# One port for two engines: a list scheduler that charges VectorE and GpSimd operations to a common resource

## The chip, the cores and the metric

The program runs on 1 core of one Trainium2 chip. A core has five engines with a queue of its own each: TensorE (PE in the rows, its weight loads PEld), VectorE (DVE), ScalarE (ACT), GpSimd (POOL) and SyncE (SP), which here only issues DMAs. Each engine takes its instructions in the order in which they stand in its queue. The metric is the device time of one execution in microseconds (us), the median of three runs.

## The reference

The kernel computes three blocks one after the other, on 4 batches of 576 tokens (2304 tokens), in fp32:

```python
A = sm(q, k_lm); Bm = sm(q_lm, k_lm); C = sm(q_lm, k)     # landmark attention, 8 heads of 64, 32 landmarks
Z = Bm^T / (norm1(Bm) * norminf(Bm) + 1e-6)
for _ in range(6): Z = 2 * Z - Z @ Bm @ Z
x = (A @ Z @ C @ v)                                        # [2304, 512]
h = x @ w_in;  x = max(0.01 * h, h) @ w_out                # first block: 512 -> 2048 -> 512
xn = x / sqrt(mean(x * x) + 1e-6) * rms_g                  # second block: 512 -> 1536 -> 512
g = xn @ w_gate; out = (silu(g) * (xn @ w_val)) @ w_out2
```

The weights arrive as 64-bit floats and are turned into fp32 on the chip.

## The kernel before

TensorE multiplies in a reduced fp32 form, so every operand is split into a high part (a rounded copy) and a low part (operand minus high part), and every product is made of three: high x high, low x high, high x low. The low parts are subtractions of two operands in SBUF; they and other elementwise work can be done by VectorE or by GpSimd.

**First block.** 8 half batches of 288 tokens (j) times 16 blocks of 128 hidden columns (f) are 128 units. `ffn1_h` makes one unit's hidden block with 6 matmuls into `ph` (line 739; the attention's last product is folded into the weights by `form_m`, line 706), ScalarE writes its high part `g_hi` (L755) and an fp32 copy `hs` (L758), and the subtraction at L761 gives the low part `g_lo`. `ffn1_y` then adds the unit to the output with 12 matmuls into `py` (L797), which wait for `g_lo`. Finished half batches go to DRAM (`y_dram`).

**Between the blocks.** `norm` loads a half batch `y_in`, squares it, sums over the 512 values (L925, L927, then a matmul at L932), takes the reciprocal root (`rr`, L938 to L952, the power on GpSimd at L943), spreads it with a matmul (`dg`, L957, L962), scales (L968) and writes it back. `prep_x` loads it again and makes seven combinations of its quarters (`tx`, L1001 to L1017) with their high and low parts (L313 and L862). `prep_w` does the same for each block of the gate and value weights (`cg`, `tt`, L890 to L897). `convert` (L337 to L400) turns a 64-bit weight piece `raw` into fp32 in three steps, the last at L374 (`cg<-raw`, `ct<-raw`) on VectorE.

**Second block.** 12 blocks of 128 hidden columns times 4 batches are 48 units (`gv`), each of seven products of 6 matmuls (L1034), by Strassen's scheme in Winograd's form. The sums of the products are five VectorE additions with an operand in PSUM: `g_hi` (L1087), `g_lo` (L1090, L1093), `ys` (L1100, L1123). TensorE's sixth product of a unit waits for L1090, its seventh for L1093. ScalarE applies Silu, and two multiplications `us` (L1108) go to DRAM. At the end 18 output tiles of 36 matmuls each (L1189) are made from `us` and `w_out2`, whose converted form comes back from DRAM as `ct` (L1149).

**What sets the order.** Every piece of work is a Python generator that yields a list of options, (engine, ns), and the events and free buffers that it needs. `Order.run` (L109) is a list scheduler: it keeps for each engine the time at which it becomes free, takes the tasks that can begin within 100 ns of the earliest, and among these the one with the smallest sum of weighted begin and due time. Where a step has several options, it takes the engine with the smallest end plus `bias`. So the order of all five queues and the choice between VectorE and GpSimd come from the lengths in `pe`, `act`, `dve`, `pool` (L152 to L181), from `bias`, and from the due times made of `unit`, `unit2` and `prep` in `PAR` (L26). The chip runs the queues in that order; semaphores make each instruction wait for its operands.

Of the kernel before, what the change touches and what calls it, by code (L numbers as in the profile page):

```python
# [26 lines left out]
    "bias": {"dve": 300, "act": 0, "pool": -700},  # L27
# [3 lines left out]
    "unit": 1900,  # L31
# [13 lines left out]
    "unit2": 2500,  # L45
    "prep": 9000,
# [3 lines left out]
class Order:  # L50
# [7 lines left out]
    GAP = 110  # L58

# [6 lines left out]
    def add(self, due, length, gen):  # L66

        task = [due - length, 0, gen, None]
        task[3] = next(gen)
        self.tasks.append(task)  # L70

    def aside(self, gen):

        self.tasks.append([self.task[0], self.now, gen, next(gen)])
        self.branches.append(self.tasks[-1])
# [33 lines left out]
    def run(self):  # L109
        while self.tasks:  # L110
            able = []
            for task in self.tasks:
                options, needs = task[3]
                t = self.ready(needs)
                if t is not None:
                    t = max(t, task[1])
                    starts = [max(t, self.engines.get(e, 0)) for e, _ in options]
# [12 lines left out]
            try:  # L130
                task[3] = task[2].send(engine)
# [4 lines left out]
            if engine is not None:  # L136
                self.engines[engine] = t + ns
            t += ns + self.GAP
            task[0] += ns + self.GAP
# [12 lines left out]
def pe(n, count=1):  # L152
    return [("pe", int(count * (n / 2.4 + 3)))]
# [13 lines left out]

def dve2(n):
    return [("dve", int(n * 0.52) + 68)]
# [6 lines left out]
def pool_dve(n):  # L176
    return pool(n) + dve(n)
# [11 lines left out]
def landmark_attention_then_two_ffns(  # L189
# [134 lines left out]
    raws, gv_f32, p2 = {}, {}, {}  # L324

# [11 lines left out]
    def convert(k, key):  # L337
# [14 lines left out]
        e = yield [("pool", 590)] + act(490) + dve2(512), []  # L352
# [14 lines left out]
        yield dve(512), room  # L367
        if what == "in":
            t = w_in_sb[f // NP][:, f % NP, :]
        else:  # L370
            tag, home = ("cg", p2["a"]) if what in ("gate", "val") else ("ct", conv)
            ct = new(tag, home, [P, 512], U32)
            t = ct[:]
# [23 lines left out]
        e = yield pool(512) + dve(512), []  # L397
# [55 lines left out]
    def chain(b, g):  # L453
# [36 lines left out]
        yield dve(2), []  # L490
# [13 lines left out]
        yield dve(2), []  # L504
        nc.vector.tensor_scalar_add(sm, sm, EPS_SM)
        rs = att_tile([P, 2], "rs")
        yield dve(2), []
        nc.vector.reciprocal(rs, sm)
        bb = att_tile([P, 2, M], "bb")
        yield dve(M + 45), []  # L510
# [7 lines left out]
        yield dve(2 * M), []  # L518
# [9 lines left out]
        yield dve(60), []  # L528
# [3 lines left out]
        yield dve(1), []  # L532
        nc.vector.tensor_scalar_add(al[:, 2:3], al[:, 2:3], -EPS_Z)
        yield dve(1), []
# [3 lines left out]
        yield dve(M + 45), []  # L538
# [99 lines left out]
    def soft_a(b, g, h):  # L638
# [25 lines left out]
        e = yield pool(SB - 60) + dve(SB), []  # L664
# [5 lines left out]
        yield dve(nb), []  # L670
        nc.vector.tensor_scalar_add(st[:, 0, :], st[:, 0, :], EPS_SM)
        yield dve(nb + 30), []
        nc.vector.reciprocal(st[:, 1, :], st[:, 0, :])
        e = yield pool(SB - 60) + dve(SB), []
# [8 lines left out]
        e = yield pool(SB) + dve(SB), []  # L683
# [41 lines left out]
    def ffn1_h(u):  # L725
# [34 lines left out]
        e = yield pool(SB) + dve(SB), []  # L760
# [95 lines left out]
    def split_steps(parts):  # L856

        for hi, lo, src, n in parts:
            e = yield act(n) + dve2(n), []
            copy(e, hi, src)  # L860
            e = yield pool(n) + dve(n), []
# [45 lines left out]
    def norm(j):  # L907
# [7 lines left out]
        e = yield act(SB) + dve(SB), [("tt", 2)]  # L915
        ss = [new("tt", p2["a"], [P, 2, SB]) for _ in range(2)]
        for d in range(KD):
            if d:
                e = yield act(SB) + dve(SB), []
# [25 lines left out]
        yield dve(3), []  # L945
        nc.vector.tensor_mul(rr[:, 2, :], rr[:, 1, :], rr[:, 1, :])
        yield dve(3), []
# [3 lines left out]
        yield dve(3), []  # L951
# [3 lines left out]
        yield dve(SB), []  # L955
# [407 lines left out]
```

## Time and profile before

| | |
|---|---|
| median of 3 runs | 917.7 us (915.56 to 921.79) |
| the profiled execution itself | 918.04 us, of which the span of the trace is 916.3 us |
| busy | PE 845.9, DVE 484.4, ACT 319.2, POOL 477.3 us |
| instructions | 6416 matmuls, 932 on VectorE, 777 on ScalarE, 476 on GpSimd |
| first block's last matmul ends, by the trace | near 453 us |
| output tiles begin, by the trace | near 763 us |

A line of waits names the waiting engine and line, the one that released it, the total in us, the number of times and the longest. Busy time of VectorE and GpSimd includes what an instruction spends waiting for something inside the engine after it has begun.

### The profile page before, as it was taken

What the parts mean: (1) busy time and instruction counts of PE and PEld (TensorE: products, weight loads), DVE (VectorE), ACT (ScalarE), POOL (GpSimd) and SP (SyncE); (2) the same over time, 40 slices, a digit from 0 to 9 for tenths busy, and PEclk for the clock granted to TensorE, in tenths of its full rate; (3) what the DMA queues carried; (4) which work ended last, traced back from release to release, by engine and by line L of the source; (5) the groups of instructions that cost most, each with busy time, mean ns of one, the idle gap of its engine ahead of it and who ended that gap; (6) DMA issues with size and microseconds to landing.
All of it is one profiled execution on the core that took longest, in us unless ns stands there. A gap on an engine that the chain in (4) does not pass through costs nothing.

```text
span 916.3 us, 16631 instructions
## 1 busy us (share of the span) xinstructions
PE 845.9 (92%) x6416; PEld 747.5 (82%) x6416; DVE 484.4 (53%) x932; ACT 319.2 (35%) x777; POOL 477.3 (52%) x476
## 2 busy tenths in 40 slices
PE   3898999999999999898866999999999979999998
PEld 1577798988888778888866999999999978888886
DVE  6983751132316515687766866666667564242420
ACT  3674543342434435544332333333332341000000
POOL 2865752322425426767455766666665556364550
PEclk8899999999999999999988999999999999999999
DMA  9957741113103105655313344444342254534330
GB/s 321 331 190 217 218 153 52 53 53 95 37 1 105 53 1 181 207 187 185 127 67 117 92 162 132 133 133 133 132 133 87 76 190 140 172 104 152 113 104 34
DMA packets 63694, 118.51 MB, mean 129 GB/s; under 512 B 5504, under 2 KB 36224, under 8 KB 63616
## 3 DMA queue, kind: packets, MB, share of 16 engines
q1 hardware_dynamic: 63616, 117.46, 39.1%
q8 instruction: 50, 0.82, 0.4%
q14 instruction: 28, 0.23, 0.1%
HBM read 81.27 MB, written 36.18 MB: 128 GB/s over the span
## 4 chain that ended last, share of the span: by engine, by line
PE 66%; DVE 15%; DMA 9%; issue 3%; POOL 3%; ACT 3%; SPq 1%; DVEq 0%; ACTq 0%; POOLq 0%
PE py L797 16%; PE py L1189 15%; PE py L1034 11%; PE ph L739 8%; PE ph L1034 5%; PE pa L1034 3%; PE pa L706 3%; DMA ct<-wo_dram 2%; DVE tt L897 2%; DVE cg L374 1%; DMA y_dram<-ys 1%; DMA raw<-w_val 1%; DMA y_in<-y_dram 1%; DVE w L862 1%; DMA raw<-w_in 1%
## 5 line engine op out<-in xcount | busy, mean ns | idle before, releaser
L797 PE MATMUL py<-g_hi,w 128*128 128x288 f32 x1024 | 211.4, 299 | 0.1
L761 POOL TENSOR_TENSOR g_lo<-hs,g_hi 128x288 fp32r<-128x288 f32 x118 | 100.2, 851 | 155.4 <-ACT hs L758 134.3
L797 PEld LDWEIGHTS py<-g_hi,w 128*128 128x128 f32 x1024 | 164.7, 189 | 7.0 <-issue 3.5
L797 PE MATMUL py<-g_lo,w 128*128 128x288 f32 x512 | 151.7, 296 | 0.0
L739 PE MATMUL ph<-at,mm 128*128 128x288 f32 x768 | 128.6, 304 | 8.6 <-ACT hs L758 6.9
L739 PEld LDWEIGHTS ph<-at,mm 128*128 128x128 f32 x768 | 108.1, 189 | 30.0 <-ACT hs L758 12.7
L755 ACT ACTIVATE g_hi<-ph 128x288 fp32r<-128x288 f32 x128 | 52.4, 409 | 141.3 <-PE py L797 127.6
L797 PEld LDWEIGHTS py<-g_lo,w 128*128 128x128 f32 x512 | 97.2, 190 | 0.2 <-POOL g_lo L761 0.2
L1108 POOL TENSOR_TENSOR us<-hs,ys 128x288 f32<-128x288 f32 x47 | 46.3, 985 | 63.3 <-ACT hs L1097 26.0
L716 DVE TENSOR_TENSOR mm<-pa,mm 128x512 fp32r<-128x512 f32 x32 | 22.0, 688 | 70.7 <-ACT mm L311 70.5
L311 ACT COPY us<-py 128x512 f32<-128x512 f32 x18 | 10.6, 588 | 133.2 <-PE py L1189 133.2
L348 ACT ACTIVATE raw<-raw 128x512 f32<-128x512 f32 x52 | 35.5, 682 | 61.4 <-DMA raw<-w_out 20.6
L1189 PE MATMUL py<-q,w 128*128 128x512 f32 x240 | 56.1, 389 | 0.0
L1034 PE MATMUL py<-w,wt 128*128 128x288 f32 x288 | 44.5, 304 | 11.7 <-DVE g_lo L1090 10.9
L358 POOL TENSOR_SCALAR raw<-raw 128x512 uint32<-128x512 uint16 x45 | 31.6, 702 | 43.1 <-DMA raw<-w_out 13.0
L862 POOL TENSOR_TENSOR w<-w,w 128x768 fp32r<-128x768 f32 x18 | 36.4, 2049 | 31.7 <-DVE w L313 31.7
L1189 PEld LDWEIGHTS py<-q,w 128*128 128x128 f32 x240 | 45.0, 188 | 9.5
L758 ACT ACTIVATE hs<-ph 128x288 f32<-128x288 f32 x128 | 52.2, 408 | 0.0
L1034 PEld LDWEIGHTS py<-w,wt 128*128 128x128 f32 x288 | 40.8, 194 | 13.2 <-DVE g_lo L1090 12.1
L1108 POOL TENSOR_TENSOR us<-ys,g_lo 128x288 f32<-128x288 f32 x47 | 44.5, 947 | 8.8 <-ACT ys L1126 8.8
L862 POOL TENSOR_TENSOR at<-w,mm 128x768 fp32r<-128x768 f32 x16 | 32.0, 2030 | 29.7 <-DVE mm L313 29.7
L1034 PE MATMUL py<-w,mm 128*128 128x288 f32 x288 | 42.9, 297 | 3.3 <-DVE g_lo L1090 3.2
(263 smaller groups left out, 1746.9 us busy)
## 6 DMA issues: line engine op xcount, KB each, us to landing
u_dram<-us SPq DMA_DIRECT2D x48, 288.0 KB, 2.5
w<-u_dram SPq DMA_DIRECT2D x9, 1536.0 KB, 7.1
raw<-w_out SPq DMA_DIRECT2D x20, 512.0 KB, 4.1
y_dram<-ys SPq DMA_DIRECT2D x64, 144.0 KB, 1.9
y_in<-y_dram SPq DMA_DIRECT2D x16, 576.0 KB, 4.2
raw<-w_gate SPq DMA_DIRECT2D x12, 512.0 KB, 4.7
raw<-w_val SPq DMA_DIRECT2D x12, 512.0 KB, 4.0
kt<-kT SPq DMA_DIRECT2D x16, 288.0 KB, 4.5
```

The costliest lines, as they stand in the source:

```text
L348: nc.scalar.activation(high.bitcast(F32), high.bitcast(F32), AF.Prelu, scale=2.0 ** -112, alpha=2.0 ** 32)
L358: nc.gpsimd.tensor_scalar(low, upper, 2.0 ** -13, -0.5 + 2.0 ** -14, op0=ALU.mult, op1=ALU.add)
L706: nc.tensor.matmul(pm[lm, :], wt_in[b, g][rows, p], w_in_sb[c][rows, 2 * g + p, :].bitcast(F32), start=True, stop=True,)
L739: nc.tensor.matmul(ph[:, :SB], w[b, c][:, g, o:o + P], x[j][:, g, :], start=(n == 0), stop=(n == 3 * NG - 1),)
L755: nc.scalar.activation(g_hi[u], ph[:, :SB], AF.Prelu, alpha=0.01)
L758: nc.scalar.activation(hs, ph[:, :SB], AF.Prelu, alpha=0.01)
L761: engine[e].tensor_sub(g_lo[u], hs, g_hi[u].bitcast(F32))
L797: nc.tensor.matmul(yacc[i][d][:, :SB], w[f][:, d * P:(d + 1) * P], x[u], start=(f == f0 and n == 0), stop=(f == f1 - 1 and n == 2),)
L862: engine[e].tensor_sub(lo, src, hi.bitcast(F32))
L1034: nc.tensor.matmul(pp[:, :SB], w[f][:, i, c * P:(c + 1) * P], x[b][1][:, k, c, :], start=(first and n == 0), stop=(n == 5), skip_group_che ...
L1108: engine[e].tensor_mul(us[0][:, h, :], sg, t[name])
L1189: nc.tensor.matmul(po[:, :DM], x[n][1][:, f, m], w[f], start=(f == 0 and i == 0), stop=(f == NF2 - 1 and i == 2),)
```

## The change

1. The scheduler gets a resource `port`. `USES` says that a step on `"pool"` or on the new kind `"dvep"` holds its engine and the port; a plain `"dve"` step holds VectorE alone. `dvep` is VectorE work without a PSUM operand (and not a reduction or transpose); it is written in place of `dve` at some 30 steps.
2. `pe` counts 0.4375 ns a column and 6.5 ns a matmul, in place of 1/2.4 and 3. A PE step that follows a PE step of the same task needs no gap of 110 ns.
3. `bias` goes from +300 (VectorE), -700 (GpSimd) to 0 and -300; `unit` from 1900 to 2400, `unit2` from 2500 to 5600, `prep` from 9000 to 7000; `convert`'s second step counts 740 ns on GpSimd and 530 on ScalarE in place of 590 and 490.
4. Gate and value pieces must be converted in the order of `gv_keys`.

```diff
-    "bias": {"dve": 300, "act": 0, "pool": -700},
+    "bias": {"dve": 0, "act": 0, "pool": -300},
-    "unit": 1900,
+    "unit": 2400,
-    "unit2": 2500,
-    "prep": 9000,
+    "unit2": 5600,
+    "prep": 7000,
+    USES = {"dvep": ("dve", "port"), "pool": ("pool", "port")}
...
-                    t = max(t, task[1])
-                    starts = [max(t, self.engines.get(e, 0)) for e, _ in options]
+                    t = max(t, task[1] - (self.GAP if task[4] == "pe" == options[0][0] else 0))
+                    starts = [
+                        max(t, *(self.engines.get(r, 0) for r in self.USES.get(e, (e,))))
+                        for e, _ in options
+                    ]
...
             if engine is not None:
-                self.engines[engine] = t + ns
+                for r in self.USES.get(engine, (engine,)):
+                    self.engines[r] = t + ns
...
-    return [("pe", int(count * (n / 2.4 + 3)))]
+    return [("pe", int(count * (n * 0.4375 + 6.5)))]
...
+def dvep(n):
+    return [("dvep", int(n * 1.04) + 67)]
 def dve2(n):
-    return [("dve", int(n * 0.52) + 68)]
+    return [("dvep", int(n * 0.52) + 68)]
 def pool_dve(n):
-    return pool(n) + dve(n)
+    return pool(n) + dvep(n)
...
-        e = yield [("pool", 590)] + act(490) + dve2(512), []
+        e = yield [("pool", 740)] + act(530) + dve2(512), []
...
-        yield dve(512), room
+        if what in ("gate", "val"):
+            if key in gv_keys[1:]:
+                room.append("cg{},{}".format(*gv_keys[gv_keys.index(key) - 1]))
+        yield dvep(512), room
...
-        e = yield pool(SB) + dve(SB), []
+        e = yield pool(SB) + dvep(SB), []
         engine[e].tensor_sub(g_lo[u], hs, g_hi[u].bitcast(F32))
```

The mathematics, the tiles and the number of matmuls stay. In the built programs 307 instructions move from GpSimd (481 to 174) and 17 from ScalarE to VectorE (934 to 1258), counted over the whole order. Of the 128 subtractions at L761, VectorE gets 106 in place of 10; of the 96 `us` products at L1108, 95 in place of 2; of the 34 low parts of 768 columns on GpSimd at the end (L862), all 34. Lines of the changed kernel that stand behind line 360 carry a number 16 higher (L761 is L777, L1090 is L1106, L374 is L390, L1108 is L1124, L862 is L878); the copies at L313 are L324.

**Where it moves, first place: VectorE in the steady part of the second block.** One unit is the five additions from `g_hi` to the second `ys`; `cg<-raw` are the conversions of the next weights, `us` the products with Silu's result. Before:

```order
L1100 TENSOR_TENSOR ys<-g_hi,py 128x288
L1123 TENSOR_TENSOR ys<-g_hi,py 128x288
L374 SCALAR_TENSOR_TENSOR cg<-raw 128x512 x2
L1087 TENSOR_TENSOR g_hi<-hs,pa 128x288
L1090 TENSOR_TENSOR g_lo<-g_hi,py 128x288
L1093 TENSOR_TENSOR g_lo<-g_lo,py 128x288
```

Now:

```order
L1139 TENSOR_TENSOR ys<-g_hi,py 128x288
L878 TENSOR_TENSOR mm<-tt,mm 128x512
L1124 TENSOR_TENSOR us<-ys,g_lo 128x288
L1103 TENSOR_TENSOR g_hi<-hs,pa 128x288
L390 SCALAR_TENSOR_TENSOR cg<-raw 128x512
L1106 TENSOR_TENSOR g_lo<-g_hi,py 128x288
L390 SCALAR_TENSOR_TENSOR cg<-raw 128x512
L1109 TENSOR_TENSOR g_lo<-g_lo,py 128x288
```

The two conversions stood together ahead of a unit's first addition; now one stands behind the first and one behind the second, and the `us` products that GpSimd did are in VectorE's queue.

**Second place: the low parts `g_lo` of the first block while the second is being prepared.** Before, on GpSimd, near the preparation of the first batch (`tx`, `q`):

```order
L1001 TENSOR_TENSOR tx<-y_in 128x576
L862 TENSOR_TENSOR q_4551<-y_in,q_4550 128x576
L358 TENSOR_SCALAR raw<-raw 128x512
L761 TENSOR_TENSOR g_lo<-hs,g_hi 128x288
L862 TENSOR_TENSOR q_4551<-tx,q_4550 128x576
```

Now, on VectorE:

```order
L390 SCALAR_TENSOR_TENSOR cg<-raw 128x512 x2
L777 TENSOR_TENSOR g_lo<-hs,g_hi 128x288
L1017 TENSOR_TENSOR tx<-y_in 128x576
L324 CAST q_4567<-y_in 128x576 x2
L777 TENSOR_TENSOR g_lo<-hs,g_hi 128x288
L1033 TENSOR_TENSOR tx<-y_in 128x576
L878 TENSOR_TENSOR q_4568<-y_in,q_4567 128x576 x3
L777 TENSOR_TENSOR g_lo<-hs,g_hi 128x288
```

The low parts that TensorE waits for now stand in one queue with the combinations of `y_in`, which wait for DMAs.

**Third place: VectorE in the last units of the second block**, where `ct` comes from DRAM and `w` is a piece of `us` loaded back. Before:

```order
L1090 TENSOR_TENSOR g_lo<-g_hi,py 128x288
L313 CAST w_989<-w_121 128x768
L1108 TENSOR_TENSOR us<-ys,g_lo 128x288
L862 TENSOR_TENSOR w_989<-w_121,w_989 128x768
L1093 TENSOR_TENSOR g_lo<-g_lo,py 128x288
```

Now:

```order
L1103 TENSOR_TENSOR g_hi<-hs,pa 128x288
L324 CAST q_4567<-ct 128x512
L1106 TENSOR_TENSOR g_lo<-g_hi,py 128x288
L1109 TENSOR_TENSOR g_lo<-g_lo,py 128x288
L878 TENSOR_TENSOR q_4568<-ct,q_4567 128x512
```

The three instructions between the two additions `g_lo` are gone from there, and copies of `ct`, which wait for a DMA, stand ahead of one of them.

## Rows read from the trace of the kernel before

**Rows 1.** The page, busy us by engine (share of the span) and instructions.

```profile
PE 845.9 (92%) x6416; PEld 747.5 (82%) x6416; DVE 484.4 (53%) x932; ACT 319.2 (35%) x777; POOL 477.3 (52%) x476
```

**Rows 2.** Busy time by stretch: length, busy by engine, clock, DMA share, GB/s.

```profile
525.50:713.70 188.20, 180.80 (x1335) 177.30 (x1334) 128.29 (x226) 62.41 (x137) 118.44 (x126) 1.00 0.39 128
366.20:454.80 88.60, 77.55 (x556) 74.08 (x555) 64.83 (x113) 39.34 (x101) 59.18 (x53) 0.98 0.53 170
454.80:525.50 70.70, 53.55 (x360) 52.27 (x360) 49.88 (x75) 22.78 (x48) 40.73 (x35) 0.88 0.30 103
713.70:771.10 57.40, 52.61 (x356) 50.16 (x354) 30.52 (x56) 18.36 (x39) 30.95 (x29) 0.97 0.48 157
0.00:366.20 366.20, 339.85 (x3206) 278.50 (x3207) 170.93 (x438) 165.74 (x436) 165.44 (x204) 0.98 0.40 129
```

**Rows 3.** TensorE's waits from 525.5 to 713.7: total us, times, longest.

```profile
PE py L1034 <- DVE g_lo L1090: 7.4, 9, 1.1
```

**Rows 4.** TensorE's waits from 366.2 to 454.8.

```profile
PE ph L739 <- ACT hs L758: 4.8, 4, 3.8
PE pa L962 <- DVE dg L957: 3.4, 2, 2.8
PE pa L932 <- POOL tt L927: 2.6, 1, 2.6
```

**Rows 5.** TensorE's waits from 454.8 to 525.5.

```profile
PE py L1034 <- DVE g_lo L1090: 7.8, 1, 7.8
PE pa L932 <- DVE tt L927: 6.6, 1, 6.6
```

**Rows 6.** TensorE's waits from 713.7 to 771.1.

```profile
PE py L1034 <- DVE g_lo L1093: 3.9, 2, 3.7
```

**Rows 7.** Timeline near 577 us: start, length, what, idle before and its releaser.

```profile
577.19 2.56 DVE L374 SCALAR_TENSOR_TENSOR cg<-raw 128x512 uint32<-128x512 uint32 x2
...
577.95 1.26 POOL L1108 TENSOR_TENSOR us<-hs,ys 128x288 f32<-128x288 f32 x1
...
580.22 0.46 DVE L1090 TENSOR_TENSOR g_lo<-g_hi,py 128x288 f32<-128x288 f32 x1
...
580.73 0.53 PE L1034 MATMUL py<-w,wt 128*128 128x288 f32 x2 [0.79 <-DVE g_lo L1090]
```

**Rows 8.** By tile: count, ns least/median/most, first and last start, shape.

```profile
L374 DVE SCALAR_TENSOR_TENSOR cg<-raw x24: 680/1292/1489, 349.2 to 696.4; 128x512 uint32<-128x512 uint32 x24
L761 DVE TENSOR_TENSOR g_lo<-hs,g_hi x10: 446/1198/1692, 99.0 to 435.8; 128x288 fp32r<-128x288 f32 x10
L761 POOL TENSOR_TENSOR g_lo<-hs,g_hi x118: 791/807/1631, 42.6 to 448.6; 128x288 fp32r<-128x288 f32 x118
L1017 DVE TENSOR_TENSOR tx<-y_in x3: 759/1954/1991, 418.1 to 492.6; 128x576 f32<-128x576 f32 x3
```

**Rows 9.** Timeline of VectorE near 478 us, two instructions in a row.

```profile
478.16 0.44 DVE L1108 TENSOR_TENSOR us<-hs,ys 128x288 f32<-128x288 f32 x1
478.53 0.44 DVE L957 TENSOR_TENSOR dg<-ident,rr 96x288 f32<-96x288 f32 x1
```

**Rows 10.** The chain that ended last, 455 to 501 us: start, length, what.

```profile
455.62 4.83 DMA y_dram<-ys
...
461.31 5.14 DMA y_in<-y_dram
...
483.03 3.16 DMA y_dram<-y_in
486.20 6.00 DMA y_in<-y_dram
...
492.68 1.87 DVE tx L1017
494.55 5.62 DVE at L862 x3
```

More of the change, by code (lines that the diff above doesn't have):

```diff
@@ L66, in add @@
     def add(self, due, length, gen):
-        task = [due - length, 0, gen, None]
+        task = [due - length, 0, gen, None, None]
         task[3] = next(gen)
@@ L72, in aside @@
     def aside(self, gen):
-        self.tasks.append([self.task[0], self.now, gen, next(gen)])
+        self.tasks.append([self.task[0], self.now, gen, next(gen), None])
         self.branches.append(self.tasks[-1])
@@ L324, in landmark_attention_then_two_ffns @@
     raws, gv_f32, p2 = {}, {}, {}
+    gv_keys = [(n, f) for f in range(NF2) for n in ("gate", "val")]
     def load_raw(k, key, tag):
@@ L372, in convert @@
             ct = new(tag, home, [P, 512], U32)
+            order.done("cg{},{}".format(*key))
             t = ct[:]
@@ L502, in chain @@
         )
-        yield dve(2), []
+        yield dvep(2), []
         nc.vector.tensor_scalar_add(sm, sm, EPS_SM)
         rs = att_tile([P, 2], "rs")
-        yield dve(2), []
+        yield dvep(2), []
         nc.vector.reciprocal(rs, sm)
         bb = att_tile([P, 2, M], "bb")
-        yield dve(M + 45), []
+        yield dvep(M + 45), []
         nc.vector.tensor_scalar_mul(bb[:, 0, :], e[:, S:S + M], rs[:, 1:2])
@@ L527, in chain @@
         nc.vector.reduce_max(al[:, 0:2], nrt, axis=AX.X)
-        yield dve(60), []
+        yield dvep(60), []
         nc.vector.tensor_scalar(
@@ L531, in chain @@
         )
-        yield dve(1), []
+        yield dvep(1), []
         nc.vector.tensor_scalar_add(al[:, 2:3], al[:, 2:3], -EPS_Z)
-        yield dve(1), []
+        yield dvep(1), []
         nc.vector.reciprocal(al[:, 3:4], al[:, 2:3])
@@ L914, in norm @@
         yield pause(2000), []
-        e = yield act(SB) + dve(SB), [("tt", 2)]
+        e = yield act(SB) + dvep(SB), [("tt", 2)]
         ss = [new("tt", p2["a"], [P, 2, SB]) for _ in range(2)]
@@ L918, in norm @@
             if d:
-                e = yield act(SB) + dve(SB), []
+                e = yield act(SB) + dvep(SB), []
             if e == "act":
@@ L943, in norm @@
         nc.gpsimd.tensor_tensor(rr[:, 1, :], rr[:, 0, :], p2["power"][:T96, :], op=ALU.pow)
-        yield dve(3), []
+        yield dvep(3), []
         nc.vector.tensor_mul(rr[:, 2, :], rr[:, 1, :], rr[:, 1, :])
-        yield dve(3), []
+        yield dvep(3), []
         nc.vector.scalar_tensor_tensor(
@@ L950, in norm @@
         )
-        yield dve(3), []
+        yield dvep(3), []
         nc.vector.scalar_tensor_tensor(
@@ L954, in norm @@
         )
-        yield dve(SB), []
+        yield dvep(SB), []
         dg = p2["a"].tile([T96, 3, T96], F32, tag="dg", bufs=1, name="dg")
```

23 lines of the change are left out of this document (12 added, 11 removed).

## The prediction

> **What bounds the kernel now.** I first read the page's busy line [rows 1]: TensorE is busy 92% of the span, VectorE and GpSimd a little over half each. That share mixes stages, so I then cut the span at five program points and read busy time by stretch [rows 2], and in each stretch what TensorE waited for. The reader should see that the idle time of TensorE lies in three places. From 366.2 us, where the first half batch is normalised, to 454.8, where the second block's first unit is summed, it is idle 88.6 - 77.6 = 11.0 us. From there to 525.5, the ninth unit, 70.7 - 53.6 = 17.1 us, and the granted clock is 0.88, so TensorE was at 1.2 GHz for about a quarter of it. In the steady part of the second block, 525.5 to 713.7, 188.2 - 180.8 = 7.4 us, and one row holds all of it: nine waits for the addition at L1090 [rows 3]. The last units, to 771.1, lose 4.8 us. The first 366.2 us lose 26.4 us, most of it at the start, where the first attention chain and the first loads must come.
>
> The timeline [rows 7] shows what such a wait is. Two conversions `cg<-raw` stand ahead of a unit's first addition on VectorE and take 1.28 us each, while GpSimd runs `us` products of 1.26 us. By tile [rows 8] the same conversion takes 0.68 us at least and 1.29 in the median. So L1090 ends late, and TensorE stands still for 0.79 us. The other rows of that group tell the same of `g_lo` (0.45 us at least on VectorE, 1.20 in the median) and `tx` (0.76 and 1.95): an instruction that reads two operands in SBUF takes a GpSimd instruction's length longer when one is running. Additions with an operand in PSUM don't. GpSimd needs 0.81 us for the `g_lo` that costs VectorE 0.45.
>
> **The change, part by part.** The sum is made against the profiled execution's own 918.04 us, 0.3 above the median.
>
> *First block, to 366.2 us.* VectorE gets 568 instructions in place of 437, two thirds of the added ones `g_lo`. Two VectorE instructions of 288 columns in a row begin 0.37 us apart [rows 9], so 131 more cost about 131 x 0.37 = 48 us: 170.9 + 48 = 219 of 366 us. GpSimd falls to about half. VectorE is not the bound, and a single `g_lo` comes sooner. What hides it is TensorE's own work; if that cover fails, it is where VectorE's queue holds a `g_lo` behind a reduction that waits for TensorE. I take 0, with 4 us less (a part of the idle 26) and 6 more (one longest wait of 3.8 us in [rows 4], one and a half times) as ends. SyncE's first 40 entries are the same loads, moved past each other in a few places: 0.
>
> *366.2 to 454.8.* Three waits make up the idle time [rows 4]. Those for `dg` (3.4) and for the sum L927 (2.6) end with VectorE or GpSimd work between two SBUF operands; the one for `hs` (4.8) ends with ScalarE, which has a conversion in its queue that waits for a weight load. The change shortens the first two and leaves the third. I take 5 us off of 6.0. The ends are 11 off (all of it) and 6 on (the same 3.8 us wait, now behind the DMA waits that stand ahead of `g_lo` on VectorE, again one and a half times).
>
> *454.8 to 525.5.* The chain [rows 10] is that of the last half batch: its output goes to DRAM, comes back, is normalised, goes to DRAM, comes back, is combined. The four DMA legs are 4.83 + 5.14 + 3.16 + 6.00 = 19.1 us of the 45 between 455.6 and 500.2, and stay. Of the rest, `tx` takes 1.87 and the three `at` 5.62 us; at the least length of such an instruction, 0.76 [rows 8], they would save 1.1 + 3.3 = 4.4. Three small `rr` steps wait likewise, about 1.1 us more. Against this the order now puts some four `us` products into that chain on VectorE, 4 x 0.37 = 1.5. Net 4 us off. TensorE's two long waits [rows 5], 7.8 and 6.6 us, are this chain's two ends and shrink but remain. Ends: 17 off, 6 on.
>
> *525.5 to 713.7.* The conversions stand apart now, behind the first and the second addition, and the `us` products that blocked them have left GpSimd: 62 of the 64 here. VectorE: 128.3 us busy, less 16 x 0.6 = 10 of blocked conversions, plus 62 x 0.37 = 23, about 141 of 188. A `cg<-raw` of 0.68 fits between the additions: the sixth product is due two products after the one that L1090 reads. GpSimd loses 62 products of at least 0.8 us (the length of a `g_lo`, the same shape [rows 8]), 50 of its 118 us, so some blocking stays. I take 6.5 of the 7.4 off. Ends: 7.4 off and a quarter more for the restart of each wait, 9; and 3 on.
>
> *713.7 to 771.1.* The wait of 3.7 us for L1093 [rows 6] came from a copy, a `us` product and a low part of 768 columns standing between the two additions. They move away, but copies of `ct`, which wait for a DMA, stand ahead of an addition in several of the last units. I set 3.9 off against as much on: 0, ends 5 off and 6 on. The output tiles behind are TensorE's own 142 us; the low parts that go from GpSimd to VectorE there are hidden by it.
>
> *The new matmul length, `bias`, due times, and the fixed order of the gate pieces* act only through the order, and are in the terms above.
>
> Sum: 0 - 5 - 4 - 6.5 + 0 = -15.5, so 918.0 - 15.5 = **902.5 us**.
>
> A rule speaks against this. The Trainium skill, "Perfetto Trace Analysis", section Optimizing Scalar/DVE Operations, says that VectorE and GpSimd share a port, so that moving operations between those two might not help. The trace agrees that they block each other, and shows by the lengths 0.45 and 0.81 us that the port is held for a shorter time after the move; by the rule alone the sum would be 0, which is the second rival.
>
> **Rivals.**
>
> *The transition was bound by the port alone.* Then nearly all idle time of the two middle stretches goes. For it: nearly every wait there but `hs` ends on VectorE or GpSimd. Against it: the 19.1 us of DMA legs, and five units of products to hide them and the work between them. Price: -6.5, -9, -13, -3: 886 us. Chance 0.15.
>
> *The stalls only change places.* A `us` product now stands on VectorE and waits for ScalarE's Silu, and later additions stand behind it; in the steady part half of the gain goes back, in the transition the DMA legs set the end. Price: -3 there, -2 elsewhere: 913 us. Against it: VectorE is three quarters full in the steady part, with slack between additions. The skill's rule would have this one. Chance 0.21.
>
> *Slower: VectorE's queue holds back the first block.* From the first normalisation to the first unit, 23 `g_lo` now stand on VectorE in one queue with 24 instructions that wait for a DMA, among them `cg<-raw` and `tx<-y_in`; before, GpSimd had most of them, and such a wait struck ScalarE instead, 3.8 us once [rows 4]. TensorE has about three units of the hidden block in hand, so a short wait is covered. If six loads come 3.8 us later than that cover, it costs 23 us, and the -6.5 of the steady part does not pay for it: 934 us. It decides from about three such waits on. For it: the four DMA legs are up to 6 us long. Against it: the scheduler places these instructions by the same loads' expected landing as before. Chance 0.11.
>
> *That the change does not do what it says* is out: the orders show 307 instructions off GpSimd.
>
> **How the numbers follow.** My forecast, the terms of the sum with their middle values, has the remaining 0.53 and by itself would lie between 893 and 911. The predicted time is its value, 902.5. About 1%, 9 us, is what a measurement of this kernel can tell from no change (three runs spread over 6 us). Faster by over 1% means below 908.8: most of the forecast (0.48 of 0.53), the first rival, and 0.05 of the second: 0.68. Slower by over 1%, above 926.9, has 0.09 of the third. The rest, 0.23, is within 1%. A range of 884 to 919 leaves out most of the third rival and the low end of the first, the outer ends of several terms added up: 2 in 10.
>
> **What would show it.** Right: `cg<-raw` near 0.7 us in the median; TensorE's waits for L1090 (now L1106) between the ninth and the forty-first unit under 2 us in total, that stretch near 181.5 us; GpSimd's busy time under 200 us, VectorE's not over 560; the stretch from the first unit's addition to the ninth near 67 us, still with two long waits for the normalisation and for L1106. Wrong: a row in which TensorE waits for `g_lo` L777 with several us; VectorE waits for DMAs that end just before; waits of VectorE for ScalarE's Silu that sum to more than the waits gone. The prediction is wrong most simply if the stretch to 366 us, which I leave as it is, changes by over 6 us.

## The result and the profile after

The changed kernel takes **890.2 us** (median of four runs, 887.5 to 891.2) against 918.0 for the kernel before in the same comparison (915.6 to 921.8): a ratio of the means of 0.9689, 95% interval 0.9649 to 0.9729. The prediction was 902.5, with a range of 884 to 919.

The page's busy line answers to [rows 1]: GpSimd has gone from 477.3 us to 137.6, VectorE from 484.4 to 540.6, and TensorE's own busy time is nearly what it was.

```profile
PE 841.3 (95%) x6416; PEld 745.8 (84%) x6416; DVE 540.6 (61%) x1256; ACT 319.1 (36%) x760; POOL 137.6 (15%) x169
```

Cut at the same program points, the stretches answer to [rows 2]. The columns are the window, its length, busy us of TensorE, its weight loads, VectorE, ScalarE and GpSimd with their instructions, the granted clock, the DMA share, GB/s.

```profile
0.00:365.60 365.60, 342.45 (x3210) 279.14 (x3211) 206.27 (x568) 167.05 (x423) 62.21 (x88) 0.98 0.40 129
365.60:448.20 82.60, 75.61 (x553) 73.82 (x553) 61.40 (x150) 39.51 (x99) 15.55 (x16) 0.98 0.54 178
448.20:512.50 64.30, 51.55 (x345) 49.94 (x344) 48.20 (x100) 20.18 (x44) 9.66 (x10) 0.89 0.34 118
512.50:692.60 180.10, 179.34 (x1346) 178.75 (x1346) 138.89 (x296) 66.61 (x148) 43.75 (x49) 1.00 0.41 134
692.60:736.30 43.70, 43.10 (x322) 42.62 (x321) 34.56 (x74) 14.07 (x32) 6.48 (x6) 1.00 0.45 152
```

The last row ends where the first output matmul starts, 736.3; before, that was 763.1, so the last units went from 49.5 to 43.7 us. (The last window of [rows 2] runs 8 us into the output tiles; the same stretch of the kernel before, cut at 763.1, is this row.)

```profile
713.70:763.10 49.40, 44.63 (x322) 43.93 (x321) 28.06 (x52) 17.29 (x37) 27.49 (x26) 0.97 0.41 135
```

The span was 26.8 us shorter at that point, by -0.6, -6.0, -6.4, -8.1 and -5.8; the output part gave 0.4 more.

TensorE's waits in the second to the fifth stretch answer to [rows 3 to 6] (who waited for whom: total us, times, longest). First, 365.6 to 448.2: the wait for the sum is gone, that for `dg` is 1.1 in place of 3.4, and the one for `hs` stands.

```profile
PE ph L755 <- ACT hs L774: 5.8, 2, 4.7
PE pa L978 <- DVE dg L973: 1.1, 1, 1.1
```

448.2 to 512.5: two long waits before; now these three, and two more of under 2 us.

```profile
PE pa L948 <- POOL tt L943: 4.6, 1, 4.6
PE pa L1050 <- ACT mm L322: 2.8, 1, 2.8
PE py L1050 <- DVE g_lo L1106: 2.4, 1, 2.4
```

512.5 to 692.6, the steady part: 0.7 us in all, this row and one of 0.2 us for L1109, where 7.4 were. In the last units TensorE is idle for 0.6 us.

```profile
PE py L1050 <- DVE g_lo L1106: 0.5, 1, 0.5
```

By tile, the rows that answer to [rows 8] (count, ns least/median/most). The conversions, the low parts and `tx` on VectorE are close to their least length in the median, where they took 1292, 1198 and 1954 ns.

```profile
L390 DVE SCALAR_TENSOR_TENSOR cg<-raw x24: 678/685/1237, 350.1 to 677.3; 128x512 uint32<-128x512 uint32 x24
L777 DVE TENSOR_TENSOR g_lo<-hs,g_hi x106: 416/458/959, 43.1 to 441.7; 128x288 fp32r<-128x288 f32 x106
L1017 DVE TENSOR_TENSOR tx<-y_in x4: 740/755/760, 412.4 to 486.0; 128x576 f32<-128x576 f32 x4
```

The timeline of VectorE in the steady part answers to [rows 7] (start, length, what). One conversion stands behind the first addition of a unit, one behind the second, each at 0.68 us, and both additions end in time.

```profile
608.65 0.45 DVE L1103 TENSOR_TENSOR g_hi<-hs,pa 128x288 f32<-128x288 f32 x1
609.03 0.68 DVE L390 SCALAR_TENSOR_TENSOR cg<-raw 128x512 uint32<-128x512 uint32 x1
609.63 0.45 DVE L1106 TENSOR_TENSOR g_lo<-g_hi,py 128x288 f32<-128x288 f32 x1
609.99 0.68 DVE L390 SCALAR_TENSOR_TENSOR cg<-raw 128x512 uint32<-128x512 uint32 x1
610.60 0.45 DVE L1109 TENSOR_TENSOR g_lo<-g_lo,py 128x288 f32<-128x288 f32 x1
```

All of this looks like the prediction's story: work left GpSimd, so VectorE is not blocked. The experiments say that, in the steady part, this is not the reason.

### The profile page after: what moved, and what is told of

It is laid out like the page before. It is cut to its first block, busy times and chain, and to the rows that moved or that the text cites. A ratio compares the mean times of both kernels' runs of the same rounds, so it can differ in the third digit from the quotient of the medians.

```text
span 889.1 us, 16491 instructions
## 1 busy us (share of the span) xinstructions
PE 841.3 (95%) x6416; PEld 745.8 (84%) x6416; DVE 540.6 (61%) x1256; ACT 319.1 (36%) x760; POOL 137.6 (15%) x169
## 5 line engine op out<-in xcount | busy, mean ns | idle before, releaser
L777 DVE TENSOR_TENSOR g_lo<-hs,g_hi 128x288 fp32r<-128x288 f32 x106 | 49.0, 462 | 85.1 <-ACT hs L774 84.6
L774 ACT ACTIVATE hs<-ph 128x288 f32<-128x288 f32 x128 | 52.0, 407 | 0.0
L1142 ACT ACTIVATE ys<-ys 128x288 f32<-128x288 f32 x48 | 21.3, 444 | 70.1 <-DVE ys L1139 70.1
L1050 PEld LDWEIGHTS py<-w,mm 128*128 128x128 f32 x288 | 39.6, 188 | 3.3 <-DVE g_lo L1106 2.6
L1205 PE MATMUL py<-q,mm 128*128 128x512 f32 x128 | 40.2, 395 | 0.0
L1113 ACT ACTIVATE hs<-ph 128x288 f32<-128x288 f32 x48 | 19.6, 408 | 49.2 <-PE ph L1050 49.1
L777 POOL TENSOR_TENSOR g_lo<-hs,g_hi 128x288 fp32r<-128x288 f32 x22 | 18.7, 852 | 102.1 <-ACT hs L774 97.1
L1116 DVE TENSOR_TENSOR ys<-g_hi,py 128x288 f32<-128x288 f32 x48 | 21.7, 451 | 21.1 <-PE py L1050 21.0
```

What stands on the lines that cost most here:

```text
L774: nc.scalar.activation(hs, ph[:, :SB], AF.Prelu, alpha=0.01)
L777: engine[e].tensor_sub(g_lo[u], hs, g_hi[u].bitcast(F32))
L1050: nc.tensor.matmul(pp[:, :SB], w[f][:, i, c * P:(c + 1) * P], x[b][1][:, k, c, :], start=(first and n == 0), stop=(n == 5), skip_group_che ...
L1113: nc.scalar.activation(sg, pp["a"][:, :SB], AF.Silu)
L1116: nc.vector.tensor_add(f32("c21", "ys"), t["u2"], pp["c"][:, :SB])
L1142: nc.scalar.activation(t["c12"], t["c12"], AF.Silu)
```

## The experiments

The change has three parts, which the experiments take apart. **M**: the move, that is the `bias` by which an operation goes to VectorE in place of GpSimd. **P**: the order knows the port, that is VectorE operations without PSUM operand and GpSimd operations book one common resource. **D**: TensorE's new matmul length, with no gap between a task's matmuls, and the new due times `unit`, `unit2`, `prep`. Two smaller parts are in none of the three: the order of the gate pieces, which every kernel but the one before, e3 and e10 has, and the new conversion lengths, which e2 takes back with the rest. D alone was not run. In the summary below every kernel is cut at the same program points: first normalisation's statistics on VectorE (n1), first, ninth and forty-first unit's first addition (u1, u9, u41), first output matmul (O). Ratios are of the means, to the kernel before in runs alternated on the same chip (medians 918.0 to 921.2), lengths are of the profiled execution.

```
                  median  ratio [95%]              to n1  n1-u1 u1-u9 u9-u41 u41-O
before             918.0  1                        366.2  88.6  70.8  188.1  49.5
after              890.2  0.9689 [0.9649, 0.9729]  365.6  82.6  64.3  180.1  43.7
e1_port_blind      931.4  1.0114 [1.0073, 1.0155]  378.3  97.5  65.1  188.5  48.6
e2_port_only       936.1  1.0190 [1.0133, 1.0246]  368.4  94.2  89.7  179.3  45.4
e3_bias_only       927.9  1.0076 [1.0046, 1.0106]  361.0  99.2  68.1  193.6  49.2
e5_old_bias        938.6  1.0186 [1.0142, 1.0230]  378.9  86.4  94.2  181.8  42.8
e4_old_pe          900.7  0.9781 [0.9742, 0.9820]  369.7  82.5  64.0  182.5  47.2
e6_old_due         918.3  0.9971 [0.9942, 0.9999]  374.8  90.8  69.3  179.1  48.6
e7_room            930.0  1.0107 [1.0071, 1.0143]  383.2  82.0  76.0  187.1  46.9
e8_long_legs       892.0  0.9679 [0.9632, 0.9726]  370.5  75.2  68.5  180.5  43.6
e9_nudge_after     898.5  0.9767 [0.9688, 0.9847]  368.5  82.5  64.0  180.1  45.8
e10_nudge_before   926.6  1.0055 [1.0022, 1.0087]  369.7  91.8  68.6  191.1  48.6
e11_norm_legs      881.9  0.9592 [0.9535, 0.9648]  366.7  77.5  59.7  180.1  43.0
e12_all_legs       886.9  0.9633 [0.9589, 0.9677]  361.2  75.6  72.5  179.6  43.4
```

**e1_port_blind.** The changed kernel, with a scheduler that knows no port.

```diff
-    USES = {"dvep": ("dve", "port"), "pool": ("pool", "port")}
+    USES = {"dvep": ("dve",), "pool": ("pool",)}
```

> The changed kernel with the resource port taken out of the scheduler: a step without PSUM operand holds VectorE alone, a GpSimd step GpSimd alone. New bias, matmul lengths, due times and order of gate pieces stay. In the order VectorE still gets 95 of 128 g_lo and 81 of 96 us products (the changed kernel 106 and 95), GpSimd 218 instructions in place of 167. If the gain of 28 us is the move of work off GpSimd (theory M), it keeps most of it: 890 to 899 us. If it is that the scheduler knows of the port (theory P), it loses most: 905 to 918, with cg<-raw back near 1.2 us in the median. If it is the matmul length and the due times (theory D): 890 to 895.

**e3_bias_only.** The kernel before, with the move alone.

```diff
-    "bias": {"dve": 300, "act": 0, "pool": -700},
+    "bias": {"dve": 0, "act": 0, "pool": -300},
```

> The kernel before with one line changed: bias 0 and -300 in place of +300 and -700. VectorE gets 97 of 128 g_lo and 71 of 96 us products, GpSimd 241 instructions in place of 474. Theory M: most of the gain is there, 892 to 902 us. Theory P: the blocking stays wherever the two run at once, so 908 to 918. Theory D: 915 to 920.

Both are slower than the kernel before, by 1.1% and 0.8%, and slower than every range named for them. Here most of the work has left GpSimd too (it keeps 220 and 243 instructions of 476), and in the steady part the conversions are short: of e1, and of e3, 16 each in that stretch.

```profile
L390 DVE SCALAR_TENSOR_TENSOR cg<-raw x16: 683/810/943, 546.3 to 712.1; 128x512 uint32<-128x512 uint32 x16
```

```profile
L374 DVE SCALAR_TENSOR_TENSOR cg<-raw x16: 676/805/939, 532.7 to 704.0; 128x512 uint32<-128x512 uint32 x16
```

Yet TensorE waits for the first addition as much as before. For e1, then for e3, from the ninth to the forty-first unit:

```profile
PE py L1050 <- DVE g_lo L1106: 6.2, 9, 0.8
```

```profile
PE py L1034 <- DVE g_lo L1090: 9.4, 14, 1.8
```

A piece of e1's timeline shows how. Two conversions and a product `us` stand in VectorE's queue ahead of the additions that TensorE needs; the conversions take 0.68 and 0.93 us, where the median before was 1.29, but there are too many of them at that place.

```profile
617.25 0.68 DVE L390 SCALAR_TENSOR_TENSOR cg<-raw 128x512 uint32<-128x512 uint32 x1
617.86 0.45 DVE L1139 TENSOR_TENSOR ys<-g_hi,py 128x288 f32<-128x288 f32 x1
618.22 0.93 DVE L390 SCALAR_TENSOR_TENSOR cg<-raw 128x512 uint32<-128x512 uint32 x1
619.08 0.44 DVE L1124 TENSOR_TENSOR us<-ys,g_lo 128x288 f32<-128x288 f32 x1
619.45 0.44 DVE L1103 TENSOR_TENSOR g_hi<-hs,pa 128x288 f32<-128x288 f32 x1
619.99 0.45 DVE L1106 TENSOR_TENSOR g_lo<-g_hi,py 128x288 f32<-128x288 f32 x1
620.50 0.79 PE L1050 MATMUL py<-w,mm 128*128 128x288 f32 x4 [0.77 <-DVE g_lo L1106]
```

This is a small part of what e1 loses. Its profiled execution is 41.7 us longer than the changed kernel's: 12.7 of them lie ahead of n1, 14.9 between n1 and u1, and 8.4 in the steady part. Between n1 and u1 TensorE waits 7.7 us for the sums `tt` and 5.3 for `g_lo` L777; what makes these late was not found out.

Without the booking the move is no gain, then. The prediction had weighed a rule of the Trainium skill ("Perfetto Trace Analysis", section Optimizing Scalar/DVE Operations) that moving work between VectorE and GpSimd might not help, since they share a port. For the move without the booking the runs agree with it: ratios 1.0114 (e1, with the new due times) and 1.0076 (e3).

**e2_port_only** and **e5_old_bias.** The order knows the port, but the work stays on GpSimd: e5 has only `bias` put back, e2 also the old due times, matmul length and costs of the conversions. (The +300 then weighs plain `dve` steps alone, since `dvep` has no entry in `bias`; GpSimd still gets every `g_lo` of the first block and every `us`.)

```diff
-    "bias": {"dve": 0, "act": 0, "pool": -300},
+    "bias": {"dve": 300, "act": 0, "pool": -700},
```

```diff
     (e2_port_only, besides)
-    "unit": 2400,   "unit2": 5600,   "prep": 7000,
+    "unit": 1900,   "unit2": 2500,   "prep": 9000,
-    return [("pe", int(count * (n * 0.4375 + 6.5)))]
+    return [("pe", int(count * (n / 2.4 + 3)))]
```

> The kernel before with the port resource, the new step kind and the order of gate pieces, but with its old bias, matmul lengths, due times and conversion lengths. GpSimd keeps the work: all 128 g_lo and all 96 us products, 517 instructions in place of 474. Theory P (knowing the port is the gain): 890 to 900 us, since the order keeps the two engines apart. Theory M (the move off GpSimd): no gain or slower, 915 to 935, since GpSimd holds the port for 0.81 us where VectorE would for 0.45. Theory D: 915 to 920.

> The changed kernel with the old bias (+300, -700) alone: port resource, new matmul lengths and due times stay, but GpSimd keeps all 128 g_lo and 96 us products (503 instructions). Theory M: the gain goes, 912 to 930 us. Theory P: it stays, 890 to 898. Theory D: it stays, 890 to 898. With e2_port_only this parts P from D.

They are the slowest kernels of the study, above every range named for them, but not in the steady part. There TensorE waits 0.5 us in e2, from the ninth to the forty-first unit:

```profile
PE py L1050 <- DVE g_lo L1106: 0.5, 1, 0.5
```

And this although a conversion takes 1.26 us there in the median, and all 96 products `us` are on GpSimd (half of them in the second row, by tile; the other half are alike):

```profile
L390 DVE SCALAR_TENSOR_TENSOR cg<-raw x16: 684/1261/1718, 562.2 to 718.4; 128x512 uint32<-128x512 uint32 x16
```

```profile
L1124 POOL TENSOR_TENSOR us<-hs,ys x48: 789/807/1262, 470.8 to 777.9; 128x288 f32<-128x288 f32 x48
```

In this piece of e2's timeline the two long conversions stand behind the additions that TensorE waits for:

```profile
604.77 0.45 DVE L1109 TENSOR_TENSOR g_lo<-g_lo,py 128x288 f32<-128x288 f32 x1 [0.35 <-PE py L1050]
605.15 1.17 DVE L390 SCALAR_TENSOR_TENSOR cg<-raw 128x512 uint32<-128x512 uint32 x1
606.75 1.27 DVE L390 SCALAR_TENSOR_TENSOR cg<-raw 128x512 uint32<-128x512 uint32 x1
```

So in these kernels a long conversion does no harm where it stands behind the additions, and a short one does where it stands ahead of them: the steady part was settled by the order, not by the move. The place of the conversions is not the whole of that order, though. e4, below, has 14 of 25 of them (`cg` and `ct`) between a unit's last addition and the next unit's first, e1 has 16 of 24 there, and TensorE waits 0.6 us for L1106 in e4 and 6.2 in e1. What else the booked order does was not found out.

The greatest loss of the two kernels is between the first and the ninth unit, 89.7 and 94.2 us; e5 also loses 12.7 us ahead of n1, e2 5.6 from n1 to u1 and 4 in the output tiles. The stretch of e2 from u1 to u9, and TensorE's longest waits in it:

```profile
462.50:552.30 89.80, 59.98 (x347) 57.32 (x347) 25.15 (x56) 26.41 (x52) 69.32 (x61) 0.75 0.23 81
```

```profile
PE pa L1050 <- ACT w L322: 12.6, 2, 6.5
PE ph L1050 <- POOL at L878: 5.9, 1, 5.9
```

GpSimd is busy 69 of 90 us there and VectorE 25; in the changed kernel it is 10 and 48 of 64. The chain that ended last in this stretch of e2 runs over GpSimd, for instance over five low parts `w` in a row, 1.4 us each, where VectorE takes 0.75 in the changed kernel:

```profile
476.87 7.04 POOL w L878 x5
```

My reading is that where both engines book one resource, what an operation costs is the time it holds it, and here the operations are a chain. The lengths, the busy times and the chain are shown; that the booking is what empties VectorE was not tried by itself. e5's longest wait there is another, 12.3 us for `dg`.

**e4_old_pe** and **e6_old_due.** Port and move as changed, and one piece of D put back: the matmul length with the pause between a task's matmuls, or the due times.

```diff
     (e4_old_pe)
-                    t = max(t, task[1] - (self.GAP if task[4] == "pe" == options[0][0] else 0))
+                    t = max(t, task[1])
-    return [("pe", int(count * (n * 0.4375 + 6.5)))]
+    return [("pe", int(count * (n / 2.4 + 3)))]
```

```diff
     (e6_old_due)
-    "unit": 2400,   "unit2": 5600,   "prep": 7000,
+    "unit": 1900,   "unit2": 2500,   "prep": 9000,
```

> The changed kernel with the matmul length of before (columns / 2.4 + 3 ns, and the usual pause between a task's matmuls) in the scheduler; port, bias, due times as changed. If the order that knows the port and the move to VectorE are the whole gain: 885 to 897 us, with the steady part (ninth to forty-first unit) at 179 to 182. If the scheduler's clock of TensorE matters (its units are planned 8% too short, so that the work on VectorE is planned to be late everywhere): above 905, the loss in the two middle stretches (n1 to u1 over 88, u1 to u9 over 70).

> The changed kernel with the due times of before (unit 1900, unit2 2500, prep 9000); port, bias and matmul length as changed. If port and move are the whole gain: 885 to 897 us. If the due times are a third part that the gain needs: above 905, mainly before the ninth unit of the second block, since due times order what competes there (first unit to ninth over 75 us), while the steady part stays at 179 to 182.

e4 falls between its two cases, 10 us above the changed kernel, and not where I had put the loss: the transition stands (82.5 and 64.0), the last units take 3.5 us more, the steady part 2.4, and 4.1 more lie ahead of n1. e6 gives the whole gain back but for 0.3%: the time to n1 is 9.2 us longer, n1 to u1 8.2, u1 to u9 5.0 (69.3 us, where I had named over 75), the last units 4.9, and only the steady part is that of the changed kernel. One of its ten runs took 2942 us; the ratio is that of the other nine, whose median is 917.8. In its last units TensorE waits for the first addition again, though the order knows the port:

```profile
PE py L1050 <- DVE g_lo L1106: 4.3, 5, 1.2
```

So the gain needs the due times as it needs the port, everywhere but in the steady part. Which of the three numbers does it was not tried, and of the 9.2 us ahead of n1 some 5 can be a difference between executions (see the first block below).

**e7_room.** Does the steady part need the port's knowledge, or just slack between VectorE's instructions?

```diff
-    USES = {"dvep": ("dve", "port"), "pool": ("pool", "port")}
+    USES = {"dvep": ("dve",), "pool": ("pool",)}
-    "bias": {"dve": 0, "act": 0, "pool": -300},
+    "bias": {"dve": 0, "dvep": -400, "act": 0, "pool": -300},
-    return [("dvep", int(n * 1.04) + 67)]
+    return [("dvep", int(n * 1.04) + 467)]
-    return [("dvep", int(n * 0.52) + 68)]
+    return [("dvep", int(n * 0.52) + 468)]
```

> The changed kernel with a scheduler that knows nothing of the port, but books 400 ns more for each VectorE operation without PSUM operand (and chooses between engines as if it didn't). If the steady part needs only slack between VectorE's instructions, so that none stands ahead of an addition that TensorE waits for: 179 to 183 us from the ninth to the forty-first unit, TensorE's waits for L1106 under 2 us there. If the order must know when GpSimd runs: 186 to 190 us there as in the order without the port, with 5 us or more of waits for L1106. The whole: 895 to 910 by the first, 920 to 935 by the second; the transition is not predicted by either.

187.1 us, by the second theory, though the waits for the first addition are a little over half of the 6.2 us of e1:

```profile
PE py L1050 <- DVE g_lo L1106: 3.9, 6, 0.9
```

The waits of 5 us or more that I had named for it did not come. The edit also moves work: GpSimd has 318 instructions, where e1 has 220. So this order shows that slack did not replace the booking, not what slack alone is worth. Over all fourteen kernels the steady part takes 179.1 to 182.5 us in the nine whose order knows the port, and 187.1 to 193.6 in the five whose order doesn't, whatever engine does the work; TensorE stands idle there for 0.2 to 1.2 us in the nine and 4.5 to 9.9 in the five. The order of the gate pieces does not part the two groups, since e1 and e7 have it. This is the one part of the change with a result of its own.

**e9_nudge_after** and **e10_nudge_before.** How far does an order's time move without any meaning?

```diff
     (e9_nudge_after)
-    "unit": 2400,   "unit2": 5600,   "prep": 7000,
+    "unit": 2350,   "unit2": 5500,   "prep": 7200,
```

```diff
     (e10_nudge_before)
-    "unit": 1900,   "unit2": 2500,   "prep": 9000,
+    "unit": 1850,   "unit2": 2400,   "prep": 9200,
```

> The changed kernel with its three due-time numbers moved by 2 to 3% (unit 2350, unit2 5500, prep 7200), which has no meaning for the port or the engines. If an order's time outside the steady part is a matter of chance that the numbers were chosen by: 895 to 920 us, stages before the ninth unit of the second block longer by 5 us or more in sum. If the parts of the change act by their meaning: 887 to 894, as the changed kernel. In both, the ninth to the forty-first unit takes 179 to 182.5 us.

> The kernel before with its due-time numbers moved by 2 to 3% (unit 1850, unit2 2400, prep 9200). If the numbers were chosen by the time and the rest is chance: 925 to 945 us. If not: 915 to 923. In both, the ninth to the forty-first unit takes 187 us or more, since this order does not know the port.

Both orders get worse, by 0.9% and 0.6%, which fits numbers that were chosen by the time, though one nudge each does not show it. The steady parts are as said. e9's total is in the range of the chance theory, but its loss is not where the chance theory had it: its middle stretches are those of the changed kernel, 2.9 us lie ahead of n1 and 2.1 in the last units (the profiled execution took 895.4 of 893.6 to 903.5). Differences of up to 1% between orders are thus no evidence for a mechanism by themselves; e6's 28 us are three times that.

**e8_long_legs**, **e11_norm_legs**, **e12_all_legs.** The scheduler takes 2.0 us for each landing in the chain of [rows 10], where the legs took 3.16 to 6.00; in the changed kernel the loads of `y_in` land in 4.8 us in the median and its stores in 3.2. In the changed kernel ScalarE and VectorE take up work whose data are not there, and hold what TensorE needs. A piece of ScalarE's and TensorE's timeline (in brackets the idle time before and its releaser), where `hs` of L774 stands behind the squares `tt` of a `y_in` that lands late:

```profile
434.71 0.44 ACT L937 ACTIVATE tt<-y_in 128x288 f32<-128x288 f32 x1 [6.06 <-DMA y_in<-y_dram]
435.06 0.39 ACT L774 ACTIVATE hs<-ph 128x288 f32<-128x288 f32 x1
435.51 1.81 PE L755 MATMUL ph<-at,mm 128*128 128x288 f32 x6 [4.66 <-ACT hs L774]
```

The edit gives the scheduler these two times. e8 has the three lines below, e11 the first two alone, e12 the three and 4.3 us for the raw weights (1.8 before).

```diff
     (norm: y_in from y_dram, ahead of the statistics)
-        yield pause(2000), []
+        yield pause(4800), []
     (norm: y_dram from y_in, normalised)
-        yield pause(2000), []
+        yield pause(3200), []
     (load_x: y_in from y_dram, ahead of the combinations; not in e11_norm_legs)
-        yield pause(2000), []
+        yield pause(4800), []
```

> The changed kernel with the landing times that its trace shows in the scheduler for the transfers of the second block's preparation: y_in 4.8 us and y_dram from y_in 3.2 us in place of 2.0. If VectorE and ScalarE lose time in the transition because they are planned to take up work whose data has not landed: first unit to ninth 58 to 62 us in place of 64.3, the whole 882 to 888. If that stretch is the chain of DMA legs itself: 64 us and 888 to 893, no difference.

> The changed kernel with the measured landing times for the two transfers of the normalisation alone (4.8 and 3.2 us in place of 2.0), and 2.0 us for the load of the normalised half batch as before. If the gain that e8_long_legs had from the first normalisation to the first unit (75.2 us in place of 82.6) comes from the normalisation's legs, and its loss behind that (68.5 in place of 64.3) from the other: 75 to 77 and 63 to 65 us, the whole 881 to 886. If the two stretches only trade work: their sum stays at 143 to 147 us, the whole 886 to 892.

> e8_long_legs with the raw weights' landing at 4.3 us as well (1.8 before). If conversions that wait for late loads hold back VectorE and ScalarE before the first unit of the second block: n1 to u1 under 75 us and the whole under 886. If an order made anew costs more than the better times give: 895 us or more.

e11 is the fastest kernel of the study, 881.9 us, ratio 0.9592 [0.9535, 0.9648], just clear of the changed kernel's 0.9649 to 0.9729 (the two were not run in one comparison): within the first case's 881 to 886, with a little less gained before u1 than it said (77.5) and more behind (59.7). The first pair of lines below is of the changed kernel, the second of e11: how long the engines stood idle until a `y_in` landed, and how often, and how long its transfers, loads and stores together, took to land (least/median/most, us).

```profile
  DMA y_in<-y_dram: 29.7, 8
DMA to landing us min/median/max: 2.8/4.2/6.7
```

```profile
  DMA y_in<-y_dram: 8.6, 3
DMA to landing us min/median/max: 2.8/4.1/6.1
```

The transfers are as long as ever; what changed is that the engines stand idle for them 8.6 us in place of 29.7, and TensorE's 5.8 us of waits for `hs` are gone. Since a nudge moves the total as much, it is this idle time and these waits, and not the total, that tie the gain to the landing times. e11's stretches from n1 to u9:

```profile
366.70:444.30 77.60, 74.74 (x559) 73.01 (x558) 57.90 (x142) 40.73 (x103) 11.52 (x12) 1.00 0.57 191
444.30:504.00 59.70, 50.35 (x340) 48.69 (x340) 49.11 (x103) 21.67 (x46) 12.05 (x13) 0.91 0.37 127
```

e8 gains 7.4 us from n1 to u1 and gives 4.2 of them back by u9; its total is that of the changed kernel, within its second case, but 68.5 us from u1 to u9 is in neither, and it starts 4.9 us late (see the first block below). e12 missed both its cases: 886.9, with n1 to u1 at 75.6, but 72.5 from u1 to u9. With a true landing time for `load_x` the stretch from u1 to u9 is 9 and 13 us longer than in e11; why stays open.

## Why the prediction was right, and where not

**First block, 0 predicted, -0.6 measured.** VectorE took 568 instructions there, as foreseen, and nothing came of it: TensorE is busy 342 of 366 us. But the term is known only to about 5 us, by a cause I did not have. The changed kernel, e8 and e11 issue the same instructions in the same order on all five engines until 384 us, and yet the stretch took 365.6, 370.5 and 366.7 us. The first 62 us already differ in the granted clock and in the transfers (the changed kernel, then e8):

```profile
0.00:62.00 62.00, 44.21 (x460) 27.52 (x464) 47.53 (x130) 38.92 (x87) 19.34 (x32) 0.89 0.88 303
```

```profile
0.00:62.00 62.00, 44.35 (x411) 27.38 (x412) 43.59 (x124) 34.78 (x80) 16.70 (x29) 0.75 0.79 267
```

**n1 to u1, -5 predicted, -6.0 measured.** Right, and in its parts: the waits for `dg` and for the sum shrank from 6.0 to 1.1 us, that for `hs` stayed. TensorE's idle time went from 11.0 to 7.0 us; the other 2 us are busy time. That both waits had a cause in the move is not shown: with the move and the old due times (e6) the stretch takes 90.8 us, and with the move alone (e3) 99.2.

**u1 to u9, -4 predicted, -6.4 measured.** The `tx` and `at` came down to 0.75 us as worked out, and of the two long waits of 14.4 us together 7.0 remain. What failed is the sentence that the four DMA legs, 19.1 us, stay and set the end. They stay, but e11 has the stretch at 59.7 us with transfers as long: they did not set its end, and part of the time went where engines queued for a landing.

**Steady part, -6.5 predicted, -8.1 measured: the size right, the reason wrong.** I wrote that the conversions stand apart now and that the `us` products that blocked them have left GpSimd, and left 0.9 us of the waits for the blocking that stays. The first half holds, the second does nothing: e2 keeps every product on GpSimd and conversions of 1.26 us, and waits 0.5 us; e1 and e3 have conversions of 0.81 and wait 6.2 and 9.4. The booking of the port in the order is the cause, by all fourteen kernels; with the wrong half of the reason, the size came out partly by luck. Of the 8.1 us, 6.6 are idle time of TensorE, which is the 6.5 that I forecast, and 1.5 are busy time. All I named as signs for it came true (conversions at 0.69, waits of 0.7 us, 180.1 us): they could not tell the two reasons apart, since the changed kernel has both the booked order and the short conversions. And a sign that I named for being wrong came true as well, waits of VectorE for ScalarE's Silu that sum to more than the waits gone (6.7 us); they cost TensorE next to nothing.

```profile
DVE us L1124 <- ACT ys L1142: 9.2, 16, 0.9
```

**Last units, 0 predicted, -5.8 measured: the term that was mis-sized**, nearly half of the 12.3 us by which the forecast was high. I set the 3.9 us of the wait for L1093 [rows 6] off against as much for copies of `ct` that wait for a DMA. The wait went and the price never came: VectorE waits for such a copy once, 0.8 us. TensorE's idle time fell by 4.2 us; another 1.5 are its busy time for as many matmuls, at a mean granted clock of 0.97 before and 1.00 now, for which the prediction had no term. The order's rows showed where these copies stand, not that their data would be late.

```profile
DVE q L324 <- DMA ct<-wo_dram: 0.8, 1, 0.8
```

**The rivals.** The transition bound by the port alone, 886 us: nearer to 890.2 than my forecast is, and wrong as a mechanism: of the 28.2 us of TensorE's idle time in the two middle stretches, nearly all of which was to go, 19.7 are still there, and knowledge of the port with the work on GpSimd makes the transition worst of all. Stalls that only change places, 913 (I called it the rule's sum of 0, which would be 918): refuted for the change as a whole. That there is no gain is true of the move without the booking (e1, e3), but the reason given is not shown: VectorE's waits for Silu in the steady part are 16.5 us in e3, and in e1 6.0, fewer than the changed kernel's 9.2. VectorE's queue behind DMA waits, 934: such waits are there, on VectorE and, longer, on ScalarE (365.6 to 512.5 us of the changed kernel):

```profile
DVE tt L939 <- DMA y_in<-y_dram: 8.4, 3, 5.2
DVE tx L1017 <- DMA y_in<-y_dram: 4.9, 2, 2.7
```

```profile
ACT tt L937 <- DMA y_in<-y_dram: 16.5, 3, 7.5
```

By e11's total they are worth about 8 us, an estimate, not the rival's 23. The row that I named for it, TensorE waiting for `g_lo` L777, is not in the changed kernel; e1 has it, 5.3 us in three waits. None of the rivals was what the experiments found: the gain needs all three parts. Move and port with the old due times are worth 0.3% (e6), the port without the move loses 1.9% (e5), the move without the port 1.1% (e1).

## What to carry to other kernels

Where two engines exclude each other, ask of a late instruction first what stands ahead of it in its queue, and only then how long that takes: a scheduler that books the shared resource put blocked conversions of 1.26 us where they cost nothing, and one that didn't put shorter ones of 0.81 us where TensorE waited for up to 0.8 us a time (e1). Before a gain is put down to one part of a change, run that part alone and the change without it; here the move and the booking were each slower alone, and signs that both theories share had confirmed the wrong one. And compare a planner's landing times with those of the trace: two numbers set from 2.0 to 4.8 and 3.2 us were worth another 1%, though a third took it back.

## What the hardware showed that I had not expected

The same order of instructions was granted 0.89 of the full clock in its first 62 us in one execution (the changed kernel), 0.83 in another (e11) and 0.75 in a third (e8). At two levels, 1.2 and 2.4 GHz, 0.89 and 0.75 are (1 - 0.89) x 2 x 62 = 14 us and 31 us at the lower one. The third moved 267 GB/s there in place of the first's 303 and reached the first normalisation 4.9 us later. What differs first between these two is TensorE's work: 46 and 36 matmuls, 7.1 and 6.1 us busy, in the first 15 us, with a granted clock of 1.00 and 305 and 306 GB/s in both. From 15 to 30 us the clock is low in both (0.63 and 0.66). From 30 to 44 us it is 0.91 and 0.50, and the transfers part as well, 293 and 248 GB/s. What set e8 back in its first 15 us, and whether clock or transfers led after that, is open. Ahead of the first normalisation, then, single profiles of this kernel cannot be told apart below some 5 us. Its steady part takes 179.6 to 180.5 us in five executions of the changed kernel and the four nearest to it (e8, e9, e11, e12).
